# One hand-ordered pipeline over 24 row tiles in place of an attention stage followed by an MLP stage

## The chip, the cores and the metric

The kernel runs on one core of a Trainium2 chip. The metric is the device time of one execution in microseconds (us); lower is better. The engines named below are TensorE (PE in the profile; its weight loads are listed as PEld), VectorE (DVE), ScalarE (ACT), GpSimd (POOL) and SyncE (SP), whose queue issues the DMA transfers.

## What is computed

A decayed linear attention over batch B = 4, H = 8 heads, S = 768 tokens and D = 64 channels a head, then a LayerNorm, a two-layer MLP with ReLU (512 to 2048 to 512) and a residual sum. The reference walks blocks of 64 tokens; both kernels use blocks of 128, which gives the same function.

```
for each block b of tokens:
    intra = (qb @ kb.T * lam**(i-j), for j <= i) @ vb
    inter = (qb * lam**(i+1)) @ kv_state
    out   = intra + inter
    kv_state = lam**block * kv_state + (kb * lam**(block-1-j)).T @ vb
x  = out, heads side by side            # [4, 768, 512]
xn = (x - mean) / sqrt(var + 1e-6) * g_ln
y  = x + relu(xn @ w_ch1) @ w_ch2
```

The 4 x 768 tokens are 24 row tiles of 128 tokens by 512 channels, six to a batch.

## The kernel before, in words

It has two stages. The attention stage loops over the 32 pairs of batch and head. For each it loads q, k and v of all six blocks (three transfers of 192 KB, lines 98 to 102), scales q and k by powers of lambda on DVE (L105, L107) and k and v on ACT (L109, L111), runs the state over the blocks (a matmul at L118, then an update on DVE at L119), transposes q and k of each block on PE (L130, L133), copies the transposes out of PSUM on ACT (L136), and for each block computes the scores (L147), masks them on DVE (L149) and accumulates two products into the output (L151, L153). ACT copies the head's output into `x_sb` (L156), which holds all 24 row tiles. With 64 channels a head, q and k fill 64 of the 128 rows or columns of a PE operand.

The MLP stage loops over the 24 row tiles: LayerNorm statistics and scaling on DVE (L182 to L192), four transposes (L197), a copy (L200), 64 matmuls of 128 columns for the first layer (L209) with a ReLU on ACT for each four of the 16 groups (L214), 16 matmuls of 512 columns for the second layer (L218), the residual sum on DVE (L223) and the store (L224). Its PSUM pool is opened after that of the attention stage is closed. The Tile scheduler sets the order of the instructions on each engine by priority; the weights are loaded and cast (L165, L166, L170, L171) where it finds room. The constants at the top include a `partition_broadcast` (L68) and an `iota` (L71) on POOL.

Of the kernel before, what the change touches and what calls it, by code (L numbers as in the profile page):

```python
# [7 lines left out]
F32 = mybir.dt.float32  # L9
BF16 = mybir.dt.bfloat16  # L10
I32 = mybir.dt.int32
AX = mybir.AxisListType
ALU = mybir.AluOpType
ACT = mybir.ActivationFunctionType


@with_exitstack
def kernel(
# [11 lines left out]
    nc = tc.nc  # L30

    B, H, S, D = q.shape
    blk = 128
    nb = S // blk
    D_model = H * D
    D_ff = moe_w_ch1.shape[1]
    eps = 1e-6

    assert D == 64

    const = ctx.enter_context(tc.tile_pool(name="const", bufs=1))
    wpool = ctx.enter_context(tc.tile_pool(name="wpool", bufs=1))
    xpool = ctx.enter_context(tc.tile_pool(name="xpool", bufs=1))
    hp = ctx.enter_context(tc.tile_pool(name="head", bufs=2))
    bt = ctx.enter_context(tc.tile_pool(name="batch", bufs=1))
    bp = ctx.enter_context(tc.tile_pool(name="blk", bufs=4))
    mp = ctx.enter_context(tc.tile_pool(name="mlp", bufs=2))
# [7 lines left out]

    tril = const.tile([blk, blk], F32)
# [3 lines left out]
        base=0, pattern=[[1, blk]], channel_multiplier=-1,  # L60
    )

    lam_sb = const.tile([1, H], F32)
    nc.sync.dma_start(lam_sb, lam[None, :])
    lnlam1 = const.tile([1, H], F32)
    nc.scalar.activation(lnlam1, lam_sb, ACT.Ln)
    lnlam = const.tile([128, H], F32)
    nc.gpsimd.partition_broadcast(lnlam, lnlam1, 128)  # L68

    io_i = const.tile([128, 1], I32)  # L70
    nc.gpsimd.iota(io_i, pattern=[[0, 1]], base=0, channel_multiplier=1)  # L71
    io_f = const.tile([128, 1], F32)
    nc.vector.tensor_copy(io_f, io_i)
    e_q = const.tile([128, 1], F32)
    nc.vector.tensor_scalar_add(e_q, io_f, 1.0)
    e_ki = const.tile([128, 1], F32)
    nc.vector.tensor_scalar(e_ki, io_f, 1.0, -1.0, op0=ALU.add, op1=ALU.mult)
    e_kv = const.tile([128, 1], F32)
    nc.vector.tensor_scalar(e_kv, io_f, -1.0, float(blk - 1), op0=ALU.mult, op1=ALU.add)

    lam_q = const.tile([128, H], F32)
    nc.scalar.activation(lam_q, lnlam, ACT.Exp, scale=e_q)
    lam_ki = const.tile([128, H], F32)
    nc.scalar.activation(lam_ki, lnlam, ACT.Exp, scale=e_ki)
    lam_kv = const.tile([128, H], F32)
    nc.scalar.activation(lam_kv, lnlam, ACT.Exp, scale=e_kv)
    lam_blk = const.tile([64, H], F32)
    nc.scalar.activation(lam_blk, lnlam[0:64], ACT.Exp, scale=float(blk))

    x_sb = xpool.tile([128, B * nb, D_model], F32)  # L90

    ps_cm = tc.tile_pool(name="aps", bufs=2, space=bass.MemoryType.PSUM)
    ps = ps_cm.__enter__()

    for b in range(B):
        for h in range(H):
            q_in = hp.tile([128, nb, D], F32, tag="qin")
            nc.sync.dma_start(q_in, q[b, h].rearrange("(t p) d -> p t d", p=128))
            k_in = hp.tile([128, nb, D], F32, tag="kin")
            nc.sync.dma_start(k_in, k[b, h].rearrange("(t p) d -> p t d", p=128))  # L100
            v_in = hp.tile([128, nb, D], F32, tag="vin")
            nc.sync.dma_start(v_in, v[b, h].rearrange("(t p) d -> p t d", p=128))

            qdec = hp.tile([128, nb, D], BF16, tag="qdec")
            nc.vector.tensor_scalar_mul(qdec, q_in, lam_q[:, h:h+1])  # L105
            kidec = hp.tile([128, nb, D], BF16, tag="kidec")
            nc.vector.tensor_scalar_mul(kidec, k_in, lam_ki[:, h:h+1])  # L107
            kkv = hp.tile([128, nb, D], BF16, tag="kkv")
            nc.scalar.mul(kkv, k_in, lam_kv[:, h:h+1])  # L109
            v_bf = hp.tile([128, nb, D], BF16, tag="vbf")  # L110
            nc.scalar.copy(v_bf, v_in)  # L111

# [142 lines left out]
```

## Time and profile before

| | us |
|---|---|
| median of 3 runs | 375.79 (375.05 to 375.95) |
| span of the profiled execution, first to last instruction | 373.3 |
| PE busy | 334.8 |
| DVE busy | 177.8 |
| ACT busy | 171.7 |
| POOL busy | 1.5 |
| attention stage on PE, first matmul to last | 20.9 to 184.2 |
| MLP stage on PE, first matmul of L209 to last of L218 | 186.1 to 369.6 |

The profiled execution's own time is given as its span alone; 375.79 - 373.3 = 2.5 us lie around it. The span runs from the first to the last instruction of the core. Busy shares are averages over stages with different limits, and a matmul's listed duration includes the time it spends in PE's pipeline, so the distance between the starts of two matmuls, not their duration, tells what each takes from PE's time.

### The profile page before, as it was taken

How to read it: one execution, taken by the hardware profiler on the slowest of the kernel's cores; microseconds unless marked ns; L12 is line 12 of the kernel's file. 1: busy time of each engine (PE TensorE's matmuls, PEld its weight loads, DVE VectorE, ACT ScalarE, POOL GpSimd, SP SyncE). 2: the span in 40 equal slices, each digit the busy share in tenths (PEclk: the TensorE clock that was granted, in tenths of full speed). 3: DMA queues.
4: the chain of work that ended last, by engine and by line, in shares of the span. 5: the costliest groups of instructions: out<-in, count | busy, mean ns of one | idle time of the engine just before them, and what ended most of it. 6: DMA issues, size and time to landing. Idle time of an engine off the chain costs nothing.

```text
span 373.3 us, 7775 instructions
## 1 busy us (share of the span) xinstructions
PE 334.8 (90%) x3112; PEld 232.4 (62%) x3136; DVE 177.8 (48%) x617; ACT 171.7 (46%) x312; POOL 1.5 (0%) x10
## 2 busy tenths in 40 slices
PE   0079999999999999999899999999999999999995
PEld 0046666666556665566577766776677766776673
DVE  0276667766666667676995404324053142220110
ACT  3156655555755555565344433444244333443332
POOL 1000000000000000000000000000000000000000
PEclk9999999999999999999999999999999999999999
DMA  9996746465664456563321000100001000100010
GB/s 179 337 270 128 155 108 153 99 152 108 144 139 98 107 114 122 134 127 100 115 86 58 30 30 30 57 30 30 30 30 59 28 30 30 58 30 28 30 58 29
DMA packets 81782, 34.32 MB, mean 92 GB/s; under 512 B 75986, under 2 KB 75986, under 8 KB 81234
## 3 DMA queue, kind: packets, MB, share of 16 engines
q1 hardware_dynamic: 81746, 33.83, 35.5%
q8 instruction: 24, 0.39, 0.5%
q14 instruction: 12, 0.10, 0.1%
HBM read 27.53 MB, written 6.29 MB: 91 GB/s over the span
## 4 chain that ended last, share of the span: by engine, by line
PE 81%; ACT 8%; issue 4%; DMA 4%; DVE 2%; SPq 0%; ACTq 0%
PE p L209 24%; PE p L218 22%; PE po L151 8%; PE po L153 7%; PE pi L147 6%; PE pk L118 5%; PE pt L130 5%; PE pt L133 4%; ACT qkT L136 3%; DMA w1f_t<-in_moe_w_ch_dram 3%; ACT xnT L200 2%; ACT v_bf L111 2%; DMA v_in<-in_v_dram 1%; PE pt L197 1%; ACT x_sb L156 1%
## 5 line engine op out<-in xcount | busy, mean ns | idle before, releaser
L209 PE MATMUL p<-xnT,w 128*128 128x128 bf16 x1536 | 91.0, 221 | 7.0 <-ACT xnT L200 7.0
L209 PEld LDWEIGHTS <-w 128*128 128x128 bf16 x1536 | 89.2, 99 | 11.2 <-issue 8.6
L214 ACT ACTIVATE hT<-p 128x512 bf16<-128x512 f32 x96 | 57.1, 595 | 68.1 <-PE p L209 68.0
L218 PE MATMUL p<-w,hT 128*128 128x512 bf16 x360 | 85.2, 379 | 1.3
L223 DVE TENSOR_TENSOR oT<-p,x_sb 128x512 f32<-128x512 f32 x24 | 16.6, 690 | 124.1 <-PE p L218 124.1
L149 DVE TENSOR_TENSOR masked<-pi,tril 128x128 bf16<-128x128 f32 x192 | 55.5, 289 | 41.5 <-PE pi L147 38.2
L130 PE MATMUL pt<-ident,qdec 128*64 128x128 bf16 x192 | 48.5, 312 | 20.9 <-DVE qdec L105 20.9
L218 PEld LDWEIGHTS <-hT 128*128 128x128 bf16 x384 | 36.6, 98 | 39.6
L147 PE MATMUL pi<-qkT 64*128 64x128 bf16 x192 | 52.8, 292 | 4.6 <-ACT qkT L136 4.5
L136 ACT COPY qkT<-pt 64x768 bf16<-64x768 bf16 x64 | 48.3, 791 | 18.2 <-PE pt L133 18.1
L119 DVE SCALAR_TENSOR_TENSOR kvs<-kvs,lam_blk,pk 64x64 bf16<-64x64 bf16 x160 | 42.5, 266 | 9.0 <-PE pk L118 8.3
L130 PEld LDWEIGHTS <-qdec 128*64 128x64 bf16 x192 | 29.2, 161 | 26.5 <-DVE qdec L105 20.9
L133 PE MATMUL pt<-ident,kidec 128*64 128x128 bf16 x192 | 45.5, 313 | 0.0
L151 PE MATMUL po<-v_bf,masked 128*128 128x64 bf16 x192 | 45.0, 235 | 0.1
L153 PE MATMUL po<-kvs,qkT 64*128 64x64 bf16 x192 | 44.4, 231 | 0.0
L118 PE MATMUL pk<-v_bf,kkv 128*64 128x64 bf16 x160 | 38.6, 258 | 0.4 <-DVE kvs L119 0.3
L111 ACT CAST v_bf<-v_in 128x384 bf16<-128x384 f32 x32 | 16.4, 511 | 41.2 <-issue 28.0
L151 PEld LDWEIGHTS <-masked 128*128 128x128 bf16 x192 | 19.9, 104 | 20.4 <-issue 4.1
L133 PEld LDWEIGHTS <-kidec 128*64 128x64 bf16 x192 | 30.2, 166 | 2.3 <-DVE kidec L107 0.2
L118 PEld LDWEIGHTS <-kkv 128*64 128x64 bf16 x160 | 22.1, 146 | 13.3 <-issue 0.2
L200 ACT COPY xnT<-pt 128x512 bf16<-128x512 bf16 x24 | 13.0, 588 | 35.2 <-PE pt L197 34.5
L153 PEld LDWEIGHTS <-qkT 64*128 64x128 bf16 x192 | 19.3, 101 | 12.2
(39 smaller groups left out, 173.7 us busy)
## 6 DMA issues: line engine op xcount, KB each, us to landing
q_in<-in_q_dram SPq DMA_DIRECT2D x32, 192.0 KB, 3.3
k_in<-in_k_dram SPq DMA_DIRECT2D x32, 192.0 KB, 3.6
v_in<-in_v_dram SPq DMA_DIRECT2D x32, 192.0 KB, 3.5
out_dram<-oT SPq DMA_DIRECT2D x24, 256.0 KB, 2.0
w1f_t<-in_moe_w_ch_dram SPq DMA_DIRECT2D x4, 1024.0 KB, 4.9
w2f_t<-in_moe_w_ch_dram SPq DMA_DIRECT2D x16, 256.0 KB, 2.9
g_ln_b<-in_moe_g_ln_dram SPq DMA_DIRECT2D x1, 256.0 KB, 3.5
lam_sb<-in_lam_dram SPq DMA_DIRECT2D x1, 0.0 KB
```

Of the source, the lines that this page charges most:

```text
L118: nc.tensor.matmul(pk, lhsT=kkv[:, bb, :], rhs=v_bf[:, bb, :])
L119: nc.vector.scalar_tensor_tensor(kvs[:, bb + 1, :], in0=kvs[:, bb, :], scalar=lam_blk_h, in1=pk, op0=ALU.mult, op1=ALU.add,)
L130: nc.tensor.matmul(pt[:, j, 0:128], lhsT=qdec[:, g, :], rhs=ident[:, 0:128], is_transpose=True, start=(j == 0), stop=False, skip_group_che ...
L133: nc.tensor.matmul(pt[:, j, 128:256], lhsT=kidec[:, g, :], rhs=ident[:, 0:128], is_transpose=True, start=False, stop=(j == GRP - 1), skip_ ...
L136: nc.any.tensor_copy(qkT[:, gg * GRP:(gg + 1) * GRP, :], pt)
L147: nc.tensor.matmul(pi, lhsT=kidecT, rhs=qdecT)
L149: nc.vector.tensor_mul(masked, pi, tril)
L151: nc.tensor.matmul(po[:, bb, :], lhsT=masked, rhs=v_b, start=(bb == 0), stop=False, skip_group_check=True)
L153: nc.tensor.matmul(po[:, bb, :], lhsT=qdecT, rhs=kvs[:, bb, :], start=False, stop=(bb == nb - 1), skip_group_check=True)
L209: nc.tensor.matmul(p1[:, ni, :], lhsT=w1[:, kk, n * 128:(n + 1) * 128], rhs=xnT[:, kk, :], start=(ni == 0 and kk == 0), stop=(ni == NG - 1 ...
L214: nc.scalar.activation(hT[:, ng * NG:(ng + 1) * NG, :], p1, ACT.Relu)
L218: nc.tensor.matmul(p2, lhsT=hT[:, kk, :], rhs=w2[:, kk, :], start=(kk == 0), stop=(kk == nKb - 1),)
```

## The change

The kernel is written anew with a fixed order (`tc.manual_schedule()`): each engine runs its instructions in the order in which the Python code issues them. The unit of work is the row tile of 128 tokens with all eight heads.

- **Loads.** One tile needs q, k and v of 128 tokens in all heads, three transfers of 256 KB (`load_tile`). Six tiles' inputs can be held. The weights come in eight transfers of 1 MB through four staging buffers and are cast by `cast_w1` (DVE and ACT, where the LayerNorm's gain is folded in) and `cast_w2` (DVE and POOL).
- **Attention of a tile** in steps: `p01` casts q and k and scales v of the *next* tile on POOL, then transposes this tile's k and q, heads in pairs (8 transposes), and copies them out of PSUM (two copies on ACT, one on DVE); the k copies go into one of two zero-padded buffers. `p2` makes the scores of the eight heads (8 matmuls), masks them in two DVE instructions and updates the state of each pair of heads (4 matmuls, one DVE instruction and, past a batch's first tile, one POOL instruction). `p3` makes the output (8 matmuls of 64 columns, 4 of 128), scales it and takes the LayerNorm statistics on DVE. `p4` transposes the centred tile (4) and copies it into the group's `xT` (ACT).
- **MLP of a group of four tiles** in 32 units of four 512-column matmuls: 16 of the first layer (`m1`, each followed by a ReLU on ACT), then 16 of the second (`m2`, four units to a tile, followed by a DVE instruction that also applies the LayerNorm's scale and the residual, and by the store).
- **The order.** The attention of tiles 0 to 3 stands alone. Then, for each of six groups, one of the 16 steps of the next group's attention stands behind every second MLP unit; the last group has no steps.

The core of the diff:

```diff
+    ctx.enter_context(tc.manual_schedule())
...
+        for name, src in (("q", q), ("k", k), ("v", v)):
+            f = inp.tile([128, H, D], F32, tag=name + "in", name=name + "in")
+            nc.sync.dma_start(f, src[b, :, c * C:(c + 1) * C, :].rearrange("h p d -> p h d"))
...
+        for kk in range(KA):
+            dst = w1[:, kk, c * W1C:(c + 1) * W1C]
+            if kk % 2 == 0:
+                nc.vector.tensor_scalar_mul(dst, f[:, kk, :], g_col[:, kk:kk + 1])
+            else:
+                nc.scalar.mul(dst, f[:, kk, :], g_col[:, kk:kk + 1])
...
+        nc.vector.tensor_copy(w2[:, c * W2K:c * W2K + hk, :], f[:, 0:hk, :])
+        nc.gpsimd.tensor_copy(w2[:, c * W2K + hk:(c + 1) * W2K, :], f[:, hk:, :])
...
-    nc.gpsimd.partition_broadcast(lnlam, lnlam1, 128)
...
+        nc.gpsimd.tensor_copy(qb, qf)
...
+        nc.gpsimd.tensor_copy(kb, kf)
...
+        nc.gpsimd.tensor_tensor(vb, vf, lam_v[:, :, None].to_broadcast([128, H, D]), op=ALU.mult)
...
+        nc.scalar.copy(kT[0:64, :, 0, :], tp[0:64, 0, :, :])
+        qT = wk.tile([128, NP, 128], BF16, tag="qT", name="qT")
+        nc.vector.tensor_copy(qT, tp[:, 1, :, :])
+        nc.scalar.copy(kT[64:128, :, 1, :], tp[64:128, 0, :, :])
...
+                nc.tensor.matmul(sc[:, i, :], lhsT=s["kT"][:, h // 2, h % 2, :], rhs=s["qT"][:, h // 2, :],
+                                 start=(i == 0), stop=(i == H // 2 - 1), skip_group_check=True)
...
+            p1_ = ps.tile([128, GT * 128], F32, tag="mm", bufs=3, name="pm1")
+            for kk in range(KA):
+                nc.tensor.matmul(p1_, lhsT=w1[:, kk, n * 128:(n + 1) * 128], rhs=xT_of[g][:, kk, :],
+                                 start=(kk == 0), stop=(kk == KA - 1))
+            nc.scalar.activation(hT[:, n, :], p1_, ACT.Relu)
...
+    for g in range(NG):
+        tiles = list(range((g + 1) * GT, min((g + 2) * GT, NT)))
+        steps = att_steps(tiles)
+        units = list(mlp_units(g))
+        for u, unit in enumerate(units):
+            if g == 0:
+                if u % 4 == 0 and u // 4 + 1 < NWC:
+                    cast_w1(u // 4 + 1)
+                if u in (6, 9, 12, 15):
+                    cast_w2(u // 3 - 2)
+            if u % 8 == 0:
+                load_next()
+            unit()
+            if u % 2 == 1 and u // 2 < len(steps):
+                f, t = steps[u // 2]
+                f(t)
+        for f, t in steps[len(units) // 2:]:
+            f(t)
```

How this moves the instructions is seen at three places. The first is PE at the passage from one piece of MLP work to the next. Before, between two tiles (`p` is PSUM, `xnb` the normalized tile, `xnT` its transpose):

```order
L218 MATMUL p_4370<-w_2878,hT 128x512
L197 LDWEIGHTS xnb [waits DVE_49]
L197 MATMUL pt<-ident,xnb 128x128
...
L209 LDWEIGHTS w_2865
L209 MATMUL p_4410<-xnT,w_2865 128x128 [waits Activation_49]
```

Now, at the passage from the first group of four tiles to the second (`pm` is PSUM, `xc` the last tile's centred output):

```order
L219 MATMUL po<-Sn,qT 128x128
L265 LDWEIGHTS hT
L265 MATMUL pm_923<-w_79,hT 128x512
...
L244 LDWEIGHTS xc [waits DVE_49]
L244 MATMUL xt<-ident,xc 128x128 [waits Activation_49]
...
L254 LDWEIGHTS w_78
L254 MATMUL pm_981<-xT,w_78 128x512 [waits Activation_49]
```

The first layer now takes the four tiles in matmuls of 512 columns, and the transposes of the group's last tile stand eight MLP matmuls behind that tile's last attention matmul (L219) and directly in front of the MLP matmuls that read their copy.

The second place is ACT in the first layer. Before, from one of the later tiles:

```order
L200 COPY xnT<-pt 128x512 [waits PE_49,Activation_49] x2
L214 ACTIVATE hT<-p_3738 128x512 [waits PE_49,Activation_49]
L186 ACTIVATE std<-mv,eps_t 128x1 [waits DVE_49]
L214 ACTIVATE hT<-p_3756 128x512 [waits PE_49]
L186 ACTIVATE std<-mv,eps_t 128x1 [waits DVE_49]
```

Now, in the second group (`tp` holds the transposed k and q, `kTp` the padded k):

```order
L256 ACTIVATE hT<-pm_1083 128x512 [waits PE_49]
L256 ACTIVATE hT<-pm_1089 128x512 [waits PE_49]
L176 COPY kTp_136<-tp 64x4x128 [waits PE_49,Activation_49]
L179 COPY kTp_136<-tp 64x4x128 [waits DVE_49]
L256 ACTIVATE hT<-pm_1120 128x512 [waits PE_49]
L256 ACTIVATE hT<-pm_1126 128x512 [waits PE_49]
L245 COPY xT<-xt 128x4x128 [waits PE_49]
```

The second k copy waits for DVE, whose copy of q reads the same PSUM tile between the two, and the ReLUs of the next units stand behind it.

The third place is SP's queue behind the first four tiles' loads, where q, k and v of tiles 4 to 6 alternate with the weights (the numbered DMAHW names are eight completion counters, used in turn):

```order
L75 DMA w1f<-in_moe_w_ch_dram 128x4x512 [waits DMAHW1_49]
L63 DMA qin<-in_q_dram 128x8x64 [waits DMAHW2_49]
L63 DMA kin<-in_k_dram 128x8x64 [waits DMAHW3_49]
L63 DMA vin<-in_v_dram 128x8x64 [waits DMAHW4_49]
L80 DMA w2f<-in_moe_w_ch_dram 128x4x512 [waits DMAHW5_49,DVE_49,Activation_49]
```

Each transfer waits until the one eight places ahead has landed, and the `w2f` transfers wait, besides, until DVE and ACT have cast the chunk that held their buffer.

## Rows read from the trace of the kernel before

**Rows 1.** The page: the span, and busy time of each engine.

```profile
span 373.3 us, 7775 instructions
PE 334.8 (90%) x3112; PEld 232.4 (62%) x3136; DVE 177.8 (48%) x617; ACT 171.7 (46%) x312; POOL 1.5 (0%) x10
```

**Rows 2.** The page: the chain that ended last, shares by engine.

```profile
PE 81%; ACT 8%; issue 4%; DMA 4%; DVE 2%; SPq 0%; ACTq 0%
```

**Rows 3.** PE's timeline near 102 us, attention stage: start us, us, engine, line.

```profile
101.97 0.31 PE L130 MATMUL pt<-ident,qdec 128*64 128x128 bf16 x1
102.08 0.31 PE L133 MATMUL pt<-ident,kidec 128*64 128x128 bf16 x1
102.19 0.31 PE L130 MATMUL pt<-ident,qdec 128*64 128x128 bf16 x1
```

**Rows 4.** Groups by form, two matmuls of 128 columns: busy us, mean ns, idle before.

```profile
L209 PE MATMUL p<-xnT,w 128*128 128x128 bf16 x1536 | 91.0, 221 | 7.0 <-ACT xnT L200 7.0
...
L147 PE MATMUL pi<-qkT 64*128 64x128 bf16 x192 | 52.8, 292 | 4.6 <-ACT qkT L136 4.5
```

**Rows 5.** Windows of 20 us, one in each stage; PEclk is the granted clock.

```profile
100.00:120.00 20.00, 19.55 (x135) 11.80 (x134) 12.36 (x52) 10.67 (x20) 0.00 (x0) 1.00 0.56 124
...
220.00:240.00 20.00, 19.34 (x210) 13.72 (x211) 5.03 (x12) 7.63 (x15) 0.00 (x0) 1.00 0.08 31
```

**Rows 6.** PE's timeline at the start of the MLP stage.

```profile
186.10 5.10 PE L209 MATMUL p<-xnT,w 128*128 128x128 bf16 x64 [0.72 <-ACT xnT L200]
```

**Rows 7.** Timeline of the MLP stage, 280 to 300 us, two tiles.

```profile
286.54 3.73 PE L209 MATMUL p<-xnT,w 128*128 128x128 bf16 x64 [0.51 <-ACT xnT L200]
...
290.11 3.62 PE L218 MATMUL p<-w,hT 128*128 128x512 bf16 x15
...
293.56 3.74 PE L209 MATMUL p<-xnT,w 128*128 128x128 bf16 x64
```

**Rows 8.** POOL's timeline, its last instructions.

```profile
1.68 0.29 POOL L58 TENSOR_SCALAR_AFFINE_SELECT tril<-tril 128x128 f32<-128x128 f32 x1
...
18.61 0.13 POOL L71 IOTA io_i<- 128x1 int32 x1 [9.89 <-issue]
```

**Rows 9.** Windows of 1 and 2 us near the start; last columns DMA share, GB/s.

```profile
0.00:2.00 2.00, 0.00 (x0) 0.00 (x0) 0.13 (x3) 1.22 (x1) 1.08 (x8) 1.00 0.00 0
...
10.00:12.00 2.00, 0.00 (x0) 0.00 (x0) 0.00 (x0) 0.51 (x2) 0.00 (x0) 1.00 1.01 348
...
24.00:26.00 2.00, 2.00 (x17) 1.19 (x14) 1.08 (x5) 0.79 (x1) 0.00 (x0) 1.00 1.27 249
...
34.00:36.00 2.00, 2.00 (x19) 1.50 (x16) 0.77 (x5) 1.33 (x3) 0.00 (x0) 1.00 1.31 235
```

**Rows 10.** Groups by form on ACT and DVE.

```profile
L214 ACT ACTIVATE hT<-p 128x512 bf16<-128x512 f32 x96 | 57.1, 595 | 68.1 <-PE p L209 68.0
...
L109 ACT ACTIVATE kkv<-k_in,lam_kv 128x384 bf16<-128x384 f32 x32 | 19.6, 615 | 1.8 <-ACT x_sb L156 1.7
...
L223 DVE TENSOR_TENSOR oT<-p,x_sb 128x512 f32<-128x512 f32 x24 | 16.6, 690 | 124.1 <-PE p L218 124.1
L182 DVE BATCH_NORM_STATS2 stats<-x_sb 128x6 f32<-128x512 f32 x24 | 16.1, 680 | 0.0
...
L200 ACT COPY xnT<-pt 128x512 bf16<-128x512 bf16 x24 | 13.0, 588 | 35.2 <-PE pt L197 34.5 <-DVE mv L184 0.7
...
L171 DVE CAST w<-w2f_t 128x512 bf16<-128x512 f32 x16 | 6.6, 411 | 0.0
...
L184 DVE BATCH_NORM_AGGREGATE mv<-stats 128x2 f32<-128x6 f32 x24 | 3.5, 174 | 0.0
```

**Rows 11.** The chain from 366 us on: start us, us, what.

```profile
366.37 3.20 PE p L218 x14
...
369.59 0.69 DVE oT L223
```

More of the change, by code (lines that the diff above doesn't have):

```diff
@@ L72 @@
[L72 to L79, printed above, removed]
+    io_i = const.tile([128, 1], I32)
+    nc.gpsimd.iota(io_i, pattern=[[0, 1]], base=1, channel_multiplier=1)
@@ new lines @@
+    e_q = const.tile([128, 1], F32)
+    nc.vector.tensor_copy(e_q, io_i)
+    e_v = const.tile([128, 1], F32)
+    nc.vector.tensor_scalar(e_v, e_q, -1.0, None, op0=ALU.mult)
+    eps_t = const.tile([128, 1], F32)
+    nc.vector.memset(eps_t, eps)
+    lamC = const.tile([128, NP, 128], F32)
+    nc.vector.memset(lamC, 0.0)
+    kTp = []
+    for i in range(2):
+        kt = const.tile([128, NP, 2, 128], BF16, name=f"kTp{i}")
+        nc.vector.memset(kt, 0.0)
+        kTp.append(kt)
+    lnlam = const.tile([128, H], F32)
@@ L81 @@
+    nc.scalar.activation(lnlam, lam_b, ACT.Ln)
+    lam_v = const.tile([128, H], F32)
+    nc.scalar.activation(lam_v, lnlam, ACT.Exp, scale=e_v)
     lam_q = const.tile([128, H], F32)
     nc.scalar.activation(lam_q, lnlam, ACT.Exp, scale=e_q)
[L83 to L88, printed above, removed]
@@ L172 @@
[L172 to L183 removed]
+    lam_c = const.tile([128, H], F32)
@@ L200 @@
-        nc.scalar.copy(xnT, pt)
-        hT = mp.tile([128, nKb, 128], BF16, tag="hT")
-        NG = 4
-        for ng in range(nKb // NG):
-            p1 = mps.tile([128, NG, 128], F32, tag="pm1", bufs=3)
-            for ni in range(NG):
-                n = ng * NG + ni
-                for kk in range(nKa):
-                    nc.tensor.matmul(
-                        p1[:, ni, :], lhsT=w1[:, kk, n * 128:(n + 1) * 128], rhs=xnT[:, kk, :],
-                        start=(ni == 0 and kk == 0), stop=(ni == NG - 1 and kk == nKa - 1),
-                        skip_group_check=True,
-                    )
-            nc.scalar.activation(hT[:, ng * NG:(ng + 1) * NG, :], p1, ACT.Relu)
@@ new lines, in p01, with att_steps, load_next @@
+    def p01(t):
+        if t + 1 < NT:
+            bf_inputs(t + 1)
+        p1(t)
+    def att_steps(tiles):
+        n = len(tiles)
+        seq = []
+        for j in range(n + 1):
+            if j < n:
+                seq.append((p01, tiles[j]))
+            if j > 0:
+                seq.append((p4, tiles[j - 1]))
+            if j < n:
+                seq.append((p2, tiles[j]))
+                seq.append((p3, tiles[j]))
+        return seq
+    next_load = [4]
+    def load_next():
+        if next_load[0] < NT:
+            load_tile(next_load[0])
+            next_load[0] += 1
@@ new lines @@
+    load_next()
+    bf_inputs(0)
+    for f, t in att_steps(list(range(GT))):
+        f(t)
+    cast_w1(0)
+    load_w2(0)
+    load_next()
+    load_w2(1)
+    load_next()
+    load_w2(2)
+    load_next()
+    load_w2(3)
+    load_next()
+    for g in range(NG):
[9 more added lines that the diff above has]
+            if u % 8 == 0:
+                load_next()
+            unit()
[3 more added lines that the diff above has]
+        for f, t in steps[len(units) // 2:]:
+            f(t)
```

280 lines of the change are left out of this document (158 added, 122 removed).

## The prediction

> **What bounds the kernel now.** I read the page first, then the chain, then PE's own rows at either stage. PE is busy for 334.8 of 373.3 us; DVE and ACT stand near half, POOL at nothing [rows 1], and of the chain that ended last 81% is PE [rows 2]. So the time is PE's. What matters is at which pace PE works. In the attention stage transposes of 128 columns start at 101.97, 102.08 and 102.19 us, 0.11 us apart [rows 3]; 128 columns at 1.2 GHz are 0.107 us. In the MLP stage 64 matmuls of 128 columns run from 286.54 to 290.11, 0.056 us apart [rows 7], which is 2.4 GHz. The groups by form say the same: a matmul of 128 columns lasts 292 ns in the attention stage and 221 ns in the MLP stage [rows 4]. The granted clock is listed as 1.00 in both stages [rows 5], so here I trust the distances. The first 64 matmuls of the MLP stage take 5.10 us [rows 6], later ones 3.73 [rows 7]: the faster level came some 3 us after dense work began.
>
> So three parts add up to the span: 21 us in which PE waits for the constants, 163 us of attention at half clock in small matmuls, and 185 us of MLP near what its columns cost. The change attacks the first two.
>
> **What it removes at the start.** POOL's `iota` runs at 18.61 us after 9.9 us in which POOL waited for nothing shown, behind the `partition_broadcast` [rows 8]; that broadcast is gone, and I put the wait down to it; were it the `iota`'s own, it would end by about 12 us, still ahead of the data below. What then sets the start is data. Nothing moves before 2.0 us; 256-byte pieces of q, k and v come at 235 to 249 GB/s, weights at 348 [rows 9]. I take 240 and 348. One tile is 3 x 256 KB = 0.786 MB, so 3.3 us; a weight chunk of 1.05 MB 3.0 us. In SP's order tiles 0 to 3 and one chunk come first: 2.0 + 4 x 3.3 + 3.0 + 1.3 for the small loads and the landing = 19.5 us. The last tile's chain follows. POOL shows no cast of 512 columns. A bound from below is DVE's 0.41 us for it [rows 10]; from above four times the 0.29 us of the 128-column `affine_select`, 1.17 us [rows 8]. I take 1.17, the engine's own row. Then, at the slow level with 0.2 us to drain: 8 transposes 1.1; the copies of k, q, k one after the other, 0.59 + 0.69 + 0.59 = 1.9 (ACT's 588 ns copy; for q no row has this form, 0.41 to 0.69 us bound it, and I take the one that reads PSUM); scores 1.1; two masks at 0.69, 1.4; output products 1.1; then scaling 0.69, statistics 0.68 and 0.17, centring 0.41, transposes 0.6, copy 0.59 [rows 10], 0.5 for the handovers: 11.4 us. ACT then scales its half of the first weight chunk, two of 512 columns at about 0.72 (615 ns for 384, scaled by an estimate). MLP work begins at 19.5 + 11.4 + 1.4 = **32 us**.
>
> **MLP.** The second layer's 16 matmuls of 512 columns take 290.11 to 293.56 = 3.45 us [rows 7]. The first layer becomes 16 such matmuls a tile instead of 64 of 128: 3.45 in place of 3.57. A tile costs 6.9 us, a group of four 27.6. The wait for each pair of tiles' copy (PE idle for 0.51 us) [rows 7] goes, but returns once a group, below.
>
> **Attention between it.** A tile has 12 transposes, 8 scores, 8 output products, and in 20 of 24 tiles 4 state and 4 inter products: 34.7 on average, 0.056 us each at the fast level, 1.94 us; a group 7.8. The 64-column ones may take half, 0.2 us a tile less at most.
>
> **New waits.** Each step has two MLP units (1.73 us) ahead of it. Four places are too tight for that. (1) The first tile of a group: between its transposes and its scores stand only two units, but ACT must finish a ReLU (0.60), then copy k, q, k (1.9) with handovers: 2.7 us, so 1.0 is exposed. (2) The ReLUs behind the second k copy start 2.7 us late; with three PSUM buffers PE runs out of them about once a group, 0.5. (3) At the group's end the last tile's scaling, statistics and centring (2.0 + handovers, 2.4) have 1.73 us of cover, then come four transposes and the copy before the next group's first matmul: 0.7 + 0.9 = 1.6. Together 3.1 us a group. (4) Elsewhere (scores to output: 0.4 + 1.4 against 1.73 + 0.4) I cost the waits at nothing; MLP matmuls cover them, and each tenth of a microsecond by which a chain grows past its two units would cost 0.1 x 3 x 20 = 6 us.
>
> POOL has four instructions a tile, 4.7 us at 1.17, against a tile's pace of 9.6; cost nothing. The Trainium skill, GPSIMD Engine Reference, section 3.1, gives 769 ns for 512 one-input elements and 4497 for 2048 two-input ones; by an estimate from that page the four take 3.8 us, and the sum stays. DVE: qT, two masks, state, scaling, statistics, centring, residual, 6 x 0.69 + 1.3 = 5.4 us a tile; ACT: 5 ReLU-like copies and two half copies, 4.5 us. Both fit.
>
> **DMA in group 0.** After tile 3 come three weight chunks, tile 4, then chunks and tiles in turn. The last w2 chunk lands at about 19.5 + 7 x 3.0 + 4 x 3.3 = 54 us and is cast by 56; the fourth m2 unit, its first reader, is due at 32 + 19 x 0.86 + 9 steps x 0.5 + 1.4 + 2 = 56. So hardly a wait; DVE, though, stands in order before that cast, with a mask behind it. I put 2 us. If weights came at 240 GB/s in their 2 KB pieces, it would be 9 us more.
>
> **Sum against the profiled span.** Start 32; group 0: 27.6 + 7.8 + 3.1 + 1.4 (clock coming up, 5.10 - 3.73) + 2 = 42; groups 1 to 4: 4 x 38.5 = 154; group 5: 27.6; end: from the last matmul, 366.37 + 3.20, to 373.3, 3.7 [rows 1, 11]. That is 259 us. The median lies 375.79 - 373.3 = 2.5 above the span before: **262 us**.
>
> **Rivals.** *Main case (0.76):* as above; 243 if no wait is seen and the clock is up at once (259 - 5 x 3.1 - 2 - 1.4 + 2.5), some 285 if the new waits are double (16 more) and weights come slowly. *The chains don't fit (0.14).* Three handovers a tile pass ACT or DVE, in order behind ReLUs and residual sums. If each of 20 tiles exposes 2 to 4 us instead of 0.8, the time is 262 + 24 to 64 = 286 to 326. For it: the change ties each engine to one order, and the scheduler of before could fill holes. Against: ACT and DVE have twice the time they need. *POOL binds (0.05).* From 9.6 / 4 = 2.4 us an instruction, twice my upper bound, POOL sets the pace; at 3.5 us it is 14 us a tile and 20 x 14 + 32 + 28 + 6 = 346. Nothing in the rows comes near.
>
> *Slower: PE stays at 1.2 GHz (0.04).* Attention work ran so for 163 us with PE listed as busy for 19.55 of 20 us [rows 5], and every second unit is now followed by such work. The Trainium skill, TensorE: Matmul & The Clock Gate, part 4, says that the faster level doesn't come with transposes. The attention stage at half clock agrees, and by that rule the interleaved groups could be held down too. Then 768 matmuls at 0.427 are 328 us and 20 tiles of attention at 3.7 are 74: 328 + 74 + 32 + 6 + 2.5 = 443. It decides from (376 - 262) / (443 - 262), 63% of the groups' work at the slow level. Against it: four in five of the groups' columns are MLP matmuls of the kind after which the level rose in 3 us [rows 6], and no wait I foresee is over 2 us.
>
> **The numbers.** Faster by over 0.3% (what a measurement here can tell): the first three cases, 0.95; the same 0.01; slower 0.04. The range 243 to 295 takes the main case and the lower third of the second.
>
> **What would show it.** First L254 matmul near 32 us; L254 and L265 matmuls 0.216 us apart from some 3 us later on; a group's end with ACT's `xT` copy as PE's releaser for about 1 us; POOL's casts near 1 us; group pitch near 38.5. Wrong if that pitch is over 44, if PE waits on DMA past 60 us, or if matmuls of 512 columns lie 0.43 us apart past 40 us.

## The result: 260.95 us, and the profile after

The changed kernel takes **260.95 us** (median of 4 runs, 258.33 to 262.12) beside 375.87 us for the kernel before (4 runs): a ratio of 0.694, 95% interval 0.690 to 0.698. The forecast was 262. The profiled execution took 260.50 us with a span of 258.8. The experiments below ran on three chips, on which the kernel before took 375.1 to 376.0 us; each ratio is to the kernel before on the same chip. Runs of one kernel lie up to 4.3 us apart, so 1 us between two medians says nothing. The ratio of one kernel below leaves out two slower executions of six, near 261.5 us.

The page of the changed kernel: span, busy time by engine, shares of the chain that ended last, then groups of instructions (busy us, mean ns of one, idle before and its releaser).

```profile
span 258.8 us, 4115 instructions
PE 223.7 (86%) x1600; PEld 122.3 (47%) x1600; DVE 137.8 (53%) x256; ACT 108.9 (42%) x207; POOL 81.0 (31%) x101
...
PE 66%; DVE 16%; ACT 9%; DMA 4%; issue 2%; POOL 1%; SPq 1%; POOLq 0%
...
L207 POOL TENSOR_TENSOR Sn<-Stmp,lamC 128x512 bf16<-128x512 f32 x16 | 20.6, 1289 | 98.9 <-DVE Stmp L206 50.4
...
L166 POOL TENSOR_TENSOR vb<-vin,lam_v 128x512 bf16<-128x512 f32 x24 | 25.9, 1079 | 6.9 <-issue 4.4
```

Against [rows 1, 2]: PE's busy time falls from 334.8 to 223.7 us and its share of the chain from 81 to 66%. The 4% of DMA in the chain is two places: the first tile's k (4.36 us from 1.71 on) and the last part of w2 in group 0 (6.55 us from 54.89 on).

Windows of the same trace, one for each stage: the attention of the first four tiles, then groups 0 to 5 (3.9 us follow them). Columns: stretch, us, busy time and count of PE, PEld, DVE, ACT and POOL, granted clock, DMA share, GB/s.

```profile
0.00:34.40 34.40, 15.96 (x140) 11.82 (x141) 21.46 (x46) 12.62 (x24) 15.13 (x26) 0.92 0.99 237
34.40:80.20 45.80, 39.22 (x265) 20.66 (x265) 27.93 (x50) 21.12 (x40) 21.38 (x23) 0.91 1.07 245
80.20:116.80 36.60, 35.24 (x268) 19.39 (x268) 21.61 (x39) 16.40 (x32) 14.58 (x18) 1.00 0.56 119
...
227.10:254.90 27.80, 27.76 (x128) 12.44 (x127) 2.25 (x3) 9.55 (x16) 0.00 (x0) 1.00 0.10 38
```

Groups 1 to 4 are even: 36.6 to 37.0 us each, of which PE is busy for 35.2. The two first stages differ: in the first PE is idle for more than half of the time, and group 0 takes 9 us more than its successors, with the DMA engines busy for nearly all of it.

PE's timeline in group 2 (start us, us, engine, line, operation, count, and in brackets the idle time before and its releaser).

```profile
116.84 1.89 PE L254 MATMUL pm<-xT,w 128*128 128x512 bf16 x8 [0.67 <-ACT xT L245]
118.57 0.39 PE L174 MATMUL tp<-ident,kb 128*128 128x128 bf16 x4
118.79 0.39 PE L174 MATMUL tp<-ident,qb 128*128 128x128 bf16 x4
...
123.33 0.40 PE L215 MATMUL po<-vb,mA 128*128 128x64 bf16 x8
123.56 1.89 PE L254 MATMUL pm<-xT,w 128*128 128x512 bf16 x8
...
128.90 1.02 PE L254 MATMUL pm<-xT,w 128*128 128x512 bf16 x4 [0.19 <-ACT hT L256]
...
152.71 0.40 PE L244 MATMUL xt<-ident,xc 128*128 128x128 bf16 x4 [0.80 <-DVE xc L229]
153.78 1.89 PE L254 MATMUL pm<-xT,w 128*128 128x512 bf16 x8 [0.67 <-ACT xT L245]
```

Eight matmuls of 512 columns start at 116.84 and the next instruction at 118.57: 0.216 us each. Four transposes take 118.57 to 118.79, 0.055 us each, where [rows 3] had 0.11. So attention work now runs at PE's faster level, with almost no idle time between steps; eight output products of 64 columns take 0.23 us (123.33 to 123.56), 0.029 each. Most of what is left of waits stands at the passage from one group to the next: 0.80 for the last tile's `xc`, 0.67 for its copy.

PE's timeline in the first two stages: the transposes of tiles 2 and 3, the first MLP matmuls, and the two long waits of group 0; then SP's waits.

```profile
18.23 0.63 PE L174 MATMUL tp<-ident,kb 128*128 128x128 bf16 x4
...
24.53 0.63 PE L174 MATMUL tp<-ident,kb 128*128 128x128 bf16 x4
...
34.41 3.79 PE L254 MATMUL pm<-xT,w 128*128 128x512 bf16 x8 [0.67 <-ACT xT L245]
...
50.91 1.02 PE L254 MATMUL pm<-xT,w 128*128 128x512 bf16 x4 [2.10 <-ACT hT L256]
...
62.21 0.59 PE L265 MATMUL pm<-w,hT 128*128 128x512 bf16 x2 [2.66 <-DVE w L95]
```

```profile
SPq L80 <- DVE w L88: 4.7, 1, 4.7
```

The tiles of the first stage follow each other at 6.3 us (18.23 to 24.53), and the MLP begins at 34.41. The first eight L254 matmuls take twice their later time, so PE was at its lower level then. At 62.21 PE has waited 2.66 us for a cast of w2's last part.

### The profile page after: what moved, and what is told of

It is laid out like the page before. It is cut to its first block, busy times and chain, and to the rows that moved or that the text cites. A ratio compares the mean times of both kernels' runs of the same rounds, so it can differ in the third digit from the quotient of the medians.

```text
span 258.8 us, 4115 instructions
## 1 busy us (share of the span) xinstructions
PE 223.7 (86%) x1600; PEld 122.3 (47%) x1600; DVE 137.8 (53%) x256; ACT 108.9 (42%) x207; POOL 81.0 (31%) x101
## 4 chain that ended last, share of the span: by engine, by line
PE 66%; DVE 16%; ACT 9%; DMA 4%; issue 2%; POOL 1%; SPq 1%; POOLq 0%
PE pm L265 28%; PE pm L254 23%; PE sc L190 4%; DVE stats L225 4%; DVE x L222 4%; PE tp L174 3%; DMA w2f<-in_moe_w_ch_dram 3%; ACT hT L256 2%; DVE mA L192 2%; ACT kTp L179 2%; PE po L215 2%; PE po L219 2%; PE xt L244 2%; DVE xc L229 2%; DMA kin<-in_k_dram 2%
## 5 line engine op out<-in xcount | busy, mean ns | idle before, releaser
L254 PE MATMUL pm<-xT,w 128*128 128x512 bf16 x384 | 92.3, 384 | 6.9 <-ACT xT L245 4.0
L265 PE MATMUL pm<-w,hT 128*128 128x512 bf16 x384 | 90.9, 382 | 3.0 <-DVE w L95 2.7
L256 ACT ACTIVATE hT<-pm 128x512 bf16<-128x512 f32 x96 | 54.4, 597 | 19.7 <-PE pm L254 19.5
L254 PEld LDWEIGHTS <-w 128*128 128x128 bf16 x384 | 36.3, 99 | 45.5 <-issue 9.2
L207 POOL TENSOR_TENSOR Sn<-Stmp,lamC 128x512 bf16<-128x512 f32 x16 | 20.6, 1289 | 98.9 <-DVE Stmp L206 50.4
L270 DVE SCALAR_TENSOR_TENSOR o<-pm,rstd,x 128x512 f32<-128x512 f32 x24 | 17.8, 741 | 48.2 <-PE pm L265 48.2
L192 DVE TENSOR_TENSOR mA<-sc,tril 128x512 bf16<-128x512 f32 x48 | 30.8, 683 | 22.3 <-PE sc L190 22.3
L166 POOL TENSOR_TENSOR vb<-vin,lam_v 128x512 bf16<-128x512 f32 x24 | 25.9, 1079 | 6.9 <-issue 4.4
L190 PE MATMUL sc<-qT,kTp 128*128 128x128 bf16 x192 | 17.8, 234 | 3.2 <-DVE qT L178 1.7
L229 DVE TENSOR_SCALAR xc<-x,mv 128x512 bf16<-128x512 f32 x24 | 18.4, 767 | 0.9
L244 PE MATMUL xt<-ident,xc 128*128 128x128 bf16 x96 | 10.0, 231 | 10.2 <-DVE xc L229 10.2
```

Of the source, the lines that this page charges most:

```text
L166: nc.gpsimd.tensor_tensor(vb, vf, lam_v[:, :, None].to_broadcast([128, H, D]), op=ALU.mult)
L190: nc.tensor.matmul(sc[:, i, :], lhsT=s["kT"][:, h // 2, h % 2, :], rhs=s["qT"][:, h // 2, :], start=(i == 0), stop=(i == H // 2 - 1), skip ...
L192: nc.vector.tensor_tensor(mA[:, half * (H // 2):(half + 1) * (H // 2), :], sc, tril[:, None, :].to_broadcast([128, H // 2, 128]), op=ALU.mult)
L207: nc.gpsimd.tensor_tensor(Sn, tmp, lamC, op=ALU.mult)
L229: nc.vector.tensor_scalar(xc, x, mv[:, 0:1], None, op0=ALU.subtract)
L254: nc.tensor.matmul(p1_, lhsT=w1[:, kk, n * 128:(n + 1) * 128], rhs=xT_of[g][:, kk, :], start=(kk == 0), stop=(kk == KA - 1))
```

## The experiments

### Is it the interleaving, or the smaller and wider work?

The change does several things at once, among them heads in pairs, 512 columns in the first layer, an earlier start, and attention between MLP matmuls. Two kernels take back the order and the width, one each; the pairs and the start were not taken back by themselves.

```diff
-            if u % 2 == 1 and u // 2 < len(steps):
-                f, t = steps[u // 2]
-                f(t)
-        for f, t in steps[len(units) // 2:]:
+        for f, t in steps:
             f(t)
```

> The same instructions, but each group's 16 attention steps stand behind its 32 MLP units instead of between them. Theory (the interleaving hides the attention's chains): the steps then run at the pace that tiles 1 to 3 show alone at the start of the changed kernel (their first transposes at 11.79, 18.23 and 24.53 us, 6.3 us a tile), 25 us a group where they now add 36.7 - 27.6 = 9.1; five such groups add about 80 us, and each first layer starts at the lower clock again (about 1.9 us more, five times): 330 to 350 us. Rival (the gain is that of pairing heads and of the 512-column matmuls, and the chains cost PE little): within 8 us of 261.

Measured: **363.81 us**, ratio to before 0.971 (0.968 to 0.974). That is 14 us above the upper end of what was expected, 330 to 350. PE's timeline of this kernel, from the attention behind the second group's MLP to the next group:

```profile
130.62 0.39 PE L174 MATMUL tp<-ident,kb 128*128 128x128 bf16 x4
130.84 0.39 PE L174 MATMUL tp<-ident,qb 128*128 128x128 bf16 x4
...
135.25 0.63 PE L174 MATMUL tp<-ident,kb 128*128 128x128 bf16 x4
135.67 0.63 PE L174 MATMUL tp<-ident,qb 128*128 128x128 bf16 x4
...
138.09 0.61 PE L244 MATMUL xt<-ident,xc 128*128 128x128 bf16 x4 [1.78 <-DVE rstd L233]
...
158.06 0.59 PE L254 MATMUL pm<-xT,w 128*128 128x512 bf16 x1 [0.67 <-ACT xT L245]
```

The attention of four tiles takes 130.62 to 158.06, 27.4 us, where the pipeline spends 36.7 - 27.6 = 9.1 on it; with 28.8 us of MLP ahead of it that is 56.2 us a group, and 5 x (56.2 - 36.7) = 98 of the 103 us lost. A group's attention was expected at 25 us. Six times 27.4 are 164 us, as much as the attention stage of the kernel before. Without the interleaving, pairs, width and the earlier start together bring 3%; the time went with the order. The clock falls with it: the four transposes at 130.62 take 0.22 us, those at 135.25 take 0.42, and between them PE alternated between small products and waits. The granted clock is 0.59 from 129.8 to 158.1.

The second kernel keeps the order and gives the first layer back its 128 columns (four matmuls a piece, as before):

```diff
-            for kk in range(KA):
-                nc.tensor.matmul(p1_, lhsT=w1[:, kk, n*128:(n+1)*128], rhs=xT_of[g][:, kk, :], ...)
+            for i in range(GT):
+                for kk in range(KA):
+                    nc.tensor.matmul(p1_[:, i*128:(i+1)*128], lhsT=w1[:, kk, n*128:(n+1)*128],
+                                     rhs=xT_of[g][:, kk, i*128:(i+1)*128], ...)
```

> Only the first layer's matmuls go back to 128 columns (64 a tile instead of 16). Theory (a matmul costs its columns at either width, as 3.57 against 3.45 us a tile in the kernel before says): 24 x 0.12 = 2.9 us more, 264 us. Rival (four times as many weight loads don't hide behind 128 columns once other work stands between; the Trainium skill, TensorE: Matmul & The Clock Gate, gives 81 ns for a matmul of 128 columns in a stream with its weight load): 1536 x (0.081 - 0.054) = 41 us more, 302 us.

Measured: **259.61 us** (259.02 to 261.2), ratio 0.693 (0.691 to 0.696): no difference from the change, where 264 was expected. PE's timeline of this kernel:

```profile
116.20 0.40 PE L244 MATMUL xt<-ident,xc 128*128 128x128 bf16 x4 [0.53 <-DVE xc L229]
116.43 2.11 PE L255 MATMUL pm<-xT,w 128*128 128x128 bf16 x32
...
123.44 1.95 PE L255 MATMUL pm<-xT,w 128*128 128x128 bf16 x32
125.23 0.39 PE L174 MATMUL tp<-ident,kb 128*128 128x128 bf16 x4
```

Two effects cancel. The 0.12 us a tile of the prediction (3.57 against 3.45) is there: 32 matmuls of 128 columns take 1.79 us (123.44 to 125.23) where eight of 512 took 1.73, so 0.12 us a tile and 3 us in all. But the passage got shorter. The first twelve matmuls now read three tiles that were copied long before, and they start 0.23 us behind the last tile's transposes (116.20 to 116.43), where the wide ones start 1.07 us behind them (152.71 to 153.78). Some 0.16 us of that comes back later (the first 32 matmuls take until 118.38); five passages at about 0.7 us are an estimated 3.4 us. So the wide matmul is worth its 3 us, and costs as much by needing all four copies at once.

### Clock or chain?

Losing the interleaving slows PE's clock and lays bare the copies. This kernel is the first of the two above with products that nobody reads, so that PE stays busy:

```diff
+    def dense(n):
+        pw = ps.tile([128, 512], F32, tag="mm", bufs=3, name="pw")
+        for i in range(n):
+            nc.tensor.matmul(pw, lhsT=warm[:, 0:128], rhs=warm, start=(i == 0), stop=(i == n - 1))
...
         for f, t in steps:
             f(t)
+            dense(3)
```

> The run with each group's attention steps behind its 32 MLP units (363.8 us) with 3 products of 512 columns from a zeroed tile added after every attention step, into a PSUM buffer that nothing reads. It splits that run's loss of about 100 us (27.4 us of attention behind each group's 28.8 us of MLP) between TensorE's lower clock and the waits of the chain. Theory 1 (mostly the waits of the chain: copies on ACT and DVE between the steps, about 6 us a tile whatever the clock): the attention takes 22 to 26 us a group, the MLP 27.7, the whole 335 to 355 us. Theory 2 (mostly the clock): the attention takes 15 us or less a group, the whole under 310 us. If the products stand in the way of the chain it comes out at 364 us or above.

Measured: **351.11 us** (349.53 to 353.74), ratio 0.936 (0.930 to 0.941). PE's timeline of a later tile:

```profile
134.60 0.39 PE L182 MATMUL tp<-ident,kb 128*128 128x128 bf16 x4
134.83 0.39 PE L182 MATMUL tp<-ident,qb 128*128 128x128 bf16 x4
...
136.38 0.40 PE L252 MATMUL xt<-ident,xc 128*128 128x128 bf16 x4 [0.52 <-DVE xc L237]
...
155.25 5.12 PE L262 MATMUL pm<-xT,w 128*128 128x512 bf16 x22
```

The transposes stay 0.055 to 0.058 us apart to the end, so the clock was held, and that returned 13 of the 103 us. The added products don't stand in the way: behind them PE still waits for DVE or ACT at three places of each tile, 0.52 us at 136.38 for instance. The attention still takes 129.47 to 155.25, 25.8 us. The rest, some 90 us, is the chain of one tile: copies, masks and statistics on ACT and DVE that nothing covers. The first theory held, in its time (335 to 355) and in its attention (22 to 26). The interleaving is worth far more as a cover for copies than as a means to hold the clock.

### The first 80 us

The loads were moved first. SP's 4.7 us of waiting (above) come from a load of w2 that needs a staging buffer; the cast that frees it stands on DVE behind the first four tiles' attention. Windows of the changed kernel (columns as above) show the transfers run dry and stop from 33.0 to 36.3 us:

```profile
22.00:26.00 4.00, 3.31 (x31) 2.73 (x31) 3.08 (x5) 0.58 (x1) 1.62 (x2) 1.00 1.07 393
...
30.00:33.00 3.00, 0.82 (x8) 0.56 (x8) 2.58 (x6) 0.29 (x1) 0.83 (x2) 0.50 0.66 133
33.00:36.30 3.30, 2.46 (x9) 0.85 (x10) 3.30 (x5) 2.53 (x5) 3.04 (x3) 0.50 0.00 0
```

```diff
     load_next()
+    load_next()
     bf_inputs(0)
...
     load_w2(2)
-    load_next()
     load_w2(3)
```

> Only SP's order changes: the loads of tile 5 go out ahead of the first w2 chunk, which waits for a staging buffer, and the last w2 chunk ahead of nothing new. In the changed kernel no DMA moves from about 33 to 36 us. Theory (group 0, 45.8 us against 36.7, is late by its weight stream): the stream closes up by about 3 us, the last w2 chunk is cast 3 us earlier, 258 us. Rival (group 0 is late because DVE and ACT hold casts in front of masks and copies): no change, 261 within 1.

Measured: **256.83 us** (256.64 to 258.39), ratio 0.686 (0.684 to 0.689). The expectation held: group 0 takes 34.40 to 76.30, 41.9 us in place of 45.8, the transfers no longer stop (219 GB/s from 33.0 to 36.3 us), and the wait of 2.66 us is gone.

```profile
76.30 1.89 PE L254 MATMUL pm<-xT,w 128*128 128x512 bf16 x7 [0.67 <-ACT xT L245]
```

Then the attention of the first four tiles, in two ways: dense products to raise the clock, and another order with two tiles in flight.

```diff
+    dense(12)
     for f, t in att_steps(list(range(GT))):
         f(t)
+        dense(3)
```

```diff
-    for f, t in att_steps(list(range(GT))):
+    for f, t in ((p01, 0), (p01, 1), (p2, 0), (p3, 0), (p2, 1), (p01, 2), (p4, 0), (p3, 1), (p2, 2),
+                 (p01, 3), (p4, 1), (p3, 2), (p2, 3), (p4, 2), (p3, 3), (p4, 3)):
         f(t)
```

> Added to the changed kernel: 12 products of 512 columns from a zeroed tile ahead of the attention of the first four tiles, and 3 after each of its 16 steps, into a PSUM buffer that nothing reads (about 60 products; none of the kernel's own work is touched). Theory (the attention of the first four tiles runs with TensorE at its lower level, 0.105 us between transposes, because TensorE is idle half of that time; the added products raise it): transposes in that stage about 0.055 us apart, the first eight L254 matmuls in 1.9 us in place of 3.8, the first L254 at 32 to 33 in place of 34.4, the whole 3 to 4 us below the changed kernel, about 257.5 us. Rival (the stage is a chain of copies and DVE work, and the added products only stand in its way): the first L254 at 36 or later, the whole 262 to 266 us.

> The changed kernel with another order of the 16 steps of the first four tiles alone: the transposes of tile t+1 and the scores of tile t+1 stand ahead of the transposes of tile t's result, so that two tiles are in flight. Theory (that stage is paced by one tile's chain after another, 6.3 us each, not by the data, of which the last is there at 22.3): the first L254 at 31 to 32 in place of 34.4, the whole 2 to 3 us shorter, 258 to 259 us. Rival (the data pace it): the first L254 at 34 still, the whole 261 us.

Measured: **260.96 us** (259.11 to 261.53, ratio 0.694, 0.691 to 0.697) and **259.47 us** (258.06 to 260.97, ratio 0.691, 0.687 to 0.696). The first missed. Its stage did what was expected: transposes 0.055 us apart, and the MLP 2.1 us earlier. PE's timeline there, and DVE's:

```profile
32.31 0.38 PE L262 MATMUL pm<-xT,w 128*128 128x512 bf16 x1
...
61.54 1.91 PE L273 MATMUL pm<-w,hT 128*128 128x512 bf16 x4 [4.11 <-DVE w L103]
```

```profile
60.80 0.69 DVE L103 CAST w<-w2f 128x1024 bf16<-128x1024 f32 x1 [4.61 <-DMA w2f<-in_moe_w_ch_dram]
```

The wait for w2's last part grew from 2.66 to 4.11 us, another of 2.0 us came up at 44 us, and the gain was gone. In the other kernel my order was no better: tile 2's transposes waited for the cast of their data until 18.29 and the MLP began at 35.12, 0.7 later than in the changed kernel (31 to 32 was expected), so its 259.47 shows nothing about two tiles in flight. Both edits of loads and clock together:

> Both edits together: the dense products in the attention of the first four tiles (alone: first L254 at 32.31 in place of 34.41, but the whole 260.96, no gain, and a wait of 4.11 us at 61.5 for the cast of w2's last part) and the loads of w2 before two tiles that are needed later (alone: 256.83). Theory (the early start was eaten by the wait for w2's last part, whose landing is set by the queue of loads, not by TensorE): with w2 ahead of those loads the start counts, the wait near 61 us is below 1.5 us, and the whole is 2 to 3 us below 256.8, about 254 to 255 us. Rival (the start is worth nothing for another reason, such as ACT's lateness in the first group): 256 to 257 us.

Measured: **259.32 us** (257.27 to 261.57, 6 runs; the profiled one is the longest), ratio 0.689 (0.687 to 0.692). Both sides missed (254 to 255, or 256 to 257): no better than the loads alone. Something else paced the first 60 us.

### The passage between groups

```diff
-            if u % 2 == 1 and u // 2 < len(steps):
+            if u % 2 == 0 and u // 2 < len(steps):
```

> Each attention step stands behind an even instead of an odd unit, so one MLP unit (0.86 us) follows the last tile's transposes before the next group's first matmul. Theory (the passage from group to group costs 1.8 us, of which the copy with its handovers is 0.9): 0.86 saved at each of five passages, 4 us, 257 us; the wait for the centring stays, some 0.8 us. Rival (the wait reappears at the group's first steps, which come one unit earlier): no change, 261 within 1.

Measured: **257.16 us** (255.69 to 259.1), ratio 0.686 (0.683 to 0.688). One more unit stands between a group's last transposes and the next group, and the wait for the copy is gone, as expected. The wait ahead of those transposes was expected to stay at 0.8 us; at three of the five passages it grew:

```profile
152.37 0.40 PE L244 MATMUL xt<-ident,xc 128*128 128x128 bf16 x4 [1.37 <-DVE xc L229]
```

There `xc` starts at 150.98 together with a POOL product and takes 1.33 us in place of 0.75; the next experiment is about that. So the mean from one group's last transposes to the next's falls only from 36.7 to 36.2 us (79.85 to 224.67, four groups), and not by the 0.86 of a unit. The profiled execution, the longest of the six, gains 1.4 us (span 257.4 against 258.8). The median gains 3.8, as forecast, but no row shows the whole of that.

### POOL beside DVE

`xc` (L229) is one DVE instruction, 0.49 us or up to 1.33. DVE's and POOL's timelines of the changed kernel:

```profile
125.43 0.49 DVE L229 TENSOR_SCALAR xc<-x,mv 128x512 bf16<-128x512 f32 x1
...
134.49 1.33 DVE L229 TENSOR_SCALAR xc<-x,mv 128x512 bf16<-128x512 f32 x1
...
151.89 0.75 DVE L229 TENSOR_SCALAR xc<-x,mv 128x512 bf16<-128x512 f32 x1
```

```profile
134.49 1.04 POOL L166 TENSOR_TENSOR vb<-vin,lam_v 128x512 bf16<-128x512 f32 x1
...
151.75 0.61 POOL L164 CAST kb<-kin 128x512 bf16<-128x512 f32 x1
```

```diff
-                nc.gpsimd.tensor_tensor(Sn, tmp, lamC, op=ALU.mult)
+                nc.vector.tensor_tensor(Sn, tmp, lamC, op=ALU.mult)
```

> The changed kernel with one instruction of each tile moved from POOL to DVE: the product of L207 (1.27 us on POOL) that makes the new state; POOL's casts of the next tile then no longer follow it. Theory (the subtraction L229 takes 0.49 us where POOL is idle and 0.75 to 1.33 us where a POOL instruction runs at the same time, because the two hold each other up; in the groups its median is 0.75): with POOL's casts at another time the median of L229 in groups 1 to 4 falls to 0.5 to 0.6 us, and the wait for it ahead of each group's last transposes (0.80 us) shrinks; DVE gets 0.7 us more a tile, which it has room for at 53%. The whole 259 to 261 us. Rival (L229's length has another cause, such as what it reads): its median stays 0.75, and the whole is 261 to 264 us by the added DVE work.

Measured: **262.33 us** (261.57 to 263.75), ratio 0.699 (0.696 to 0.702). The mechanism is shown, the gain isn't there: all 16 of the `xc` in groups 1 to 4 now take 0.48 or 0.49 us, at other times than POOL's work, but the product added to DVE delays them by as much as they got shorter: the wait ahead of the last transposes is 0.85 us, where it was 0.80. This edit together with the earlier steps was not run.

```profile
153.22 0.49 DVE L229 TENSOR_SCALAR xc<-x,mv 128x512 bf16<-128x512 f32 x1
```

```profile
153.77 0.40 PE L244 MATMUL xt<-ident,xc 128*128 128x128 bf16 x4 [0.85 <-DVE xc L229]
```

In the changed kernel both start together at 134.49, POOL's product ends at 135.53 and DVE's instruction 0.29 us later; at the passage POOL's cast ends at 152.36 and DVE's instruction 0.28 us later. So DVE seems held until POOL is done. The Trainium skill, SBUF — State Buffer, "Who interferes with whom", describes it: some DVE operations, casts and operations with a scalar operand among them, can use a port pair that DVE shares with GpSimd, and the one that comes second is blocked for the whole of the other's instruction. The rows agree.

### All together, and what held the front

> The edits that shortened a stage together: the loads of w2 earlier (256.83 alone), the attention steps one unit earlier (257.16 alone), the dense products in the first four tiles' attention, and the cast of w1's first part moved into that stage (behind the transposes of its last tile) so that w2's first load no longer waits for it. Theory (the gains lie in different stages and add): 260.9 less 4.1, 3.8 and 2 to 3 gives 250 to 251, a little more if the cast stands in the chain of the first four tiles: 250 to 253 us. Rival (they gain on the same waits of the first group): 254 to 256 us.

> The version with all that helped, and the casts of w1's other three parts on DVE alone instead of half on ACT. Theory (in the first group ACT is late with the ReLUs because two casts of 0.67 us stand between them, three times; TensorE waits about 2 us for it near 51 us): that wait goes to under 1 us, and the whole is 1 to 2 us below the version with all that helped. Rival (DVE, at 28 us of the 46 us of the first group and slowed beside POOL, becomes the late one): the whole is the same or up to 3 us above it.

The first kernel has the loads of w2, the earlier steps and the dense products from above, and this; the second has the second diff too.

```diff
-    for f, t in att_steps(list(range(GT))):
+    for i, (f, t) in enumerate(att_steps(list(range(GT)))):
         f(t)
         dense(3)
+        if i == 11:
+            cast_w1(0)
...
-    cast_w1(0)
     load_w2(0)
```

```diff
-            if kk % 2 == 0:
+            if kk % 2 == 0 or c > 0:
                 nc.vector.tensor_scalar_mul(dst, f[:, kk, :], g_col[:, kk:kk + 1])
```

Measured: **257.48 us** (256.49 to 257.85, ratio 0.686, 0.684 to 0.688) and **257.63 us** (257.12 to 258.36, ratio 0.687, 0.685 to 0.689). The first lies above both of its ranges (250 to 253, or 254 to 256): nothing added up, and sharing the casts otherwise changed nothing. PE's, ACT's and DVE's timelines of the first of them, at its longest wait:

```profile
58.50 1.87 PE L273 MATMUL pm<-w,hT 128*128 128x512 bf16 x4 [4.33 <-ACT hT L264]
```

```profile
57.67 0.29 ACT L239 ACTIVATE std<-mv,eps_t 128x1 f32<-128x1 f32 x1 [9.04 <-DVE mv L235]
57.87 1.07 ACT L264 ACTIVATE hT<-pm 128x512 bf16<-128x512 f32 x2
```

```profile
55.40 0.69 DVE L103 CAST w<-w2f 128x1024 bf16<-128x1024 f32 x1 [4.84 <-DMA w2f<-in_moe_w_ch_dram]
```

PE's row names ACT. Followed back, ACT's ReLUs stand behind a square root that waits for DVE's statistics, and these stand behind a cast that waits 4.84 us for w2's third part to land. One late transfer holds three engines, since each works in order. So the last run moves nothing but the loads:

```diff
     load_w2(0)
-    load_next()
     load_w2(1)
     load_next()
     load_w2(2)
     load_w2(3)
+    load_next()
     load_next()
```

> The version with all that helped, with one thing changed: the order of the loads, in which two parts of w2 follow each other ahead of tile 6, and the other two ahead of tile 7. Theory (the first 60 us are paced by the transfers: whatever TensorE gains ahead of that is lost again in the wait for w2's later parts near 59 us, because 8 tiles and both weights, 14.7 MB, stand ahead of w2's last part in one queue that is busy all the time): 0.79 MB less stands ahead of it, which at the 230 to 260 GB/s of that stretch is 3.0 to 3.4 us; the wait of 4.33 us near 58.5 falls to about 1 us, and the whole is 253.5 to 255 us in place of 257.5. If tile 7 is then late, the wait moves to its transposes, near 62 to 65 us, and half of the gain is left. Rival (the wait is ACT's and DVE's, which have casts of weights between the ReLUs and masks in the first group): it stays at 4 us, and the whole at 257 to 258 us.

Measured: **253.21 us** (252.78 to 253.42, 5 runs), ratio to before 0.674 (0.672 to 0.677): 3% below the changed kernel, and the fastest here. DVE's cast of w2's third part, and PE:

```profile
51.88 0.69 DVE L103 CAST w<-w2f 128x1024 bf16<-128x1024 f32 x1 [4.66 <-DMA w2f<-in_moe_w_ch_dram]
```

```profile
54.99 1.82 PE L273 MATMUL pm<-w,hT 128*128 128x512 bf16 x4 [3.14 <-ACT hT L264]
...
74.19 0.40 PE L252 MATMUL xt<-ident,xc 128*128 128x128 bf16 x4 [1.38 <-DVE xc L237]
```

The cast comes 3.5 us earlier, the group's end 3.9 (74.19 against 78.13), the whole 4.3 (ratio 0.674 against 0.686). So the transfers pace the front, and not the casts' share of ACT and DVE. The wait shrank to 3.14 us, not to 1: the cast still stands ahead of statistics that don't need it. Putting it later in DVE's order was not tried.

## Why the prediction was right, step by step

The forecast was 262 and the time 260.95, but its terms were off by more than the total, in both directions: 6.2 us too little ahead of group 1, 7.0 too much in groups 1 to 4. That they cancel to 1 us is luck. The mechanism (PE bound, attention between MLP matmuls at the faster level, a wait at each passage) is what the rows show.

| term | forecast | profiled | difference |
|---|---|---|---|
| MLP begins | 32 | 34.4 | +2.4 |
| group 0 | 42 | 45.8 | +3.8 |
| groups 1 to 4 | 154 | 147.0 | -7.0 |
| group 5 | 27.6 | 27.8 | +0.2 |
| end | 3.7 | 3.9 | +0.2 |
| span | 259 | 258.8 | |

**MLP begins at 32.** The step that failed is "data of tile 3 at 19.5, then one chain of 11.4". The data were later (POOL takes tile 3's v at 21.31) and weren't what the last tile waited for: its transposes stand at 24.53 behind tile 2's steps, at 6.3 us a tile. From there to the first L254 it is 9.9 us. The forecast has 10.2 for these steps (11.4 less the cast's 1.17) and 1.4 more for ACT's scaling, for which the first matmul didn't wait. The dense products show that 2.1 us of this stage is PE's lower level, which I had priced into the last chain but not into the three ahead of it.

**Group 0, 42.** The terms "2 us for w2" and "last w2 chunk at 54, cast by 56" were too small: the cast starts at 61.47. I had the queue never pausing: its data were 1.8 us late already at tile 3 (21.3 for 19.5), and then it ran thin from 30 us on and stood still for 3.3 us, for the staging buffer. ACT's delay (2.10 us at 50.91) was not in the sum: its ReLUs stand behind two scalings of w1 and a copy that waits for DVE. The load experiments put a measured price on this term: 3.9 us of group 0 for the pause (the first load edit), and 3.9 at the group's end, 4.3 in the whole, for one tile's data ahead of w2's last three parts (the last run). One sign of being wrong, PE waiting on DMA past 60 us, nearly came: the 2.66 us up to 62.21 are a cast that waited for w2's last transfer.

**Groups 1 to 4, 38.5 each.** Mechanism right, two sizes off. *Attention*: 7.8 forecast, about 6.9 found; the 64-column products take half, the option that the prediction named and didn't take. *Waits*: 3.1 forecast, 2.2 found. The passage is 0.80 + 0.67 + handover, 1.8 against 1.6 (at two of the five the first wait is 0.53); the wait between a group's first transposes and scores is 0.2 us, not 1.0, and PSUM's 0.2, not 0.5. Of the first, 0.27 us are `qT`'s copy, which takes 0.42 us where I took 0.69; the rest I didn't take apart.

**POOL and DVE.** POOL's bound held for three of its four instructions (0.63, 0.63 and 1.08 us on average, against 1.17); the state product takes 1.29, so a tile costs 3.6 us, under the 4.7. That POOL costs nothing needs one reservation: it lengthens DVE's `xc` by up to 0.84 us, and `xc` is what the passage waits for.

**The rivals.** "The chains don't fit" is what the first experiment shows at full size, 364 us: without cover the chains and the lower clock cost 98 us, with two units of cover between steps they cost 2 us a group. "PE stays at 1.2 GHz" didn't come about: the granted clock reads 1.00 in groups 1 to 5, transposes 0.055 us apart. What it was based on is real, as the kernel without interleaving shows (transposes 0.105 us apart at 135.25). The Trainium skill, TensorE: Matmul & The Clock Gate, part 4, says that transposes don't bring the faster level. These rows fit that, and so do the dense products that kept it up; but the stretch holds other small products and waits too, so it isn't shown for transposes alone.

## What to carry to other kernels

Small products whose results pass through other engines want large matmuls between them: the attention of four tiles cost 27.4 us in a stretch of its own and 9 between MLP matmuls, and of the 103 us that this order is worth about 13 are the clock, the rest the cover of copies. A total that doesn't move can be two effects that cancel, as with the narrow matmuls: look at the rows of both. When an edit shortens a stage and the total doesn't move, look for the wait that grew by the same amount, and follow it back past the engine that the row names: an in-order engine that waits for a transfer hands its wait on to every queue behind it. Order the loads by when their last byte is needed; one tile's data ahead of a weight cost more than any instruction here.

## What the runs showed that I had not expected

- Columns of a dense stream cost only 3 to 4% more in 128s than in 512s (1.79 against 1.73 us), and the order of the narrow ones won that back: 259.61 us against 260.95.
- Products of 64 columns start 0.029 us apart, half of 128 columns.
- The granted clock in a window isn't always the pace: 1.00 from 22 to 26 us of the changed kernel, where the transposes at 24.53 start 0.105 us apart. Distances between starts are the better witness.
- DVE's `xc` takes 0.49 us alone and 0.75 to 1.33 beside a POOL instruction.
- The rate of the loads goes with their pieces. Over the first 80 us of the changed kernel 41,326 of 45,737 packets are under 512 bytes; windows in which weights come (22 to 26 us) show 393 GB/s, those with q, k and v alone (16 to 18 us) 220. The Trainium skill, DMA: Bandwidth & Descriptors, "Specifications", names 512 bytes as the least size for full rate; q, k and v come in 256-byte rows.
